# Four edits to a fused RWKV and two-layer MLP kernel: product order, place of the weight tests, form of mish, and the planner's distances

## The chip, the cores and the metric

The kernel runs on one core of a Trainium2 chip. The metric is device time of that core in microseconds (us): the median of three runs of the kernel before is 1250.47 us (1247.47 to 1251.25). Five engines work side by side, each with its own instruction stream in program order: PE (matrix products), DVE (vector), ACT (scalar functions), POOL and SP, which here issues all data movement. They meet through semaphores.

## The reference, cut to what matters

Three stages follow each other: a recurrence over 768 steps for 4 batches x 8 heads with a 40 x 40 state, a dense layer pair with mish, and a second pair with h - tanh(h). Weights come in float64.

```python
for t in range(S):                      # S = 768
    y[:, :, t] = einsum('bhd,bhde->bhe', rt, state)
    Sa = einsum('bhde,bhe->bhd', state, at)
    state_decay = state * wt[:, :, None, :] - einsum('bhd,bhe->bhde', Sa, bt)
    state = state_decay + einsum('bhd,bhe->bhde', vt, kt)
# tokens 3072, model width 320, hidden width 2048
h = x @ w_in;  x1 = (h * tanh(log1p(exp(h)))) @ w_out        # first layer
h = x1 @ w_in2; out = (h - tanh(h)) @ w_out2                 # second layer
```

## The kernel before

The work is in two phases. **Phase 1** takes the 768 steps as 12 chunks of 64. For each chunk and batch, `a0` and `a1` prepare scaled keys and a triangular matrix, `inv` inverts it, and `steps` makes the chunk's outputs and the new state with small matrix products: z, then the u products (`put` and `pu`, 16 of them for each chunk and batch, 768 in all, each of 64 rows of the array), then the state update. The 256 tokens of a finished chunk go through `moe1`, the first layer: 16 hidden blocks ("units"), in groups of four. `unit_in` makes h of a unit in PSUM (8 products), ACT takes a sigmoid of it into `th`, DVE multiplies h by it into `u`; `act` then runs an arctangent and a sine over the four units' `th`, and `unit_out` forms the activation, splits it in a high and a low part (`gh`, `gl`) and makes 6 products into y. There are 192 units. Arctangent and sine lie in different function tables, so each of the 48 groups brings table loads on ACT. Only two PSUM buffers hold h.

Beside this, phase 1 converts the float64 weights of the second layer in 88 pieces of 128 x 128 (`second_pieces`, `convert`, tile `raw`) and writes them to DRAM. With each piece `small` runs a test whether a value lies outside the range that the conversion can treat: an absolute value, a Relu with a sum into a column of `bad`, and the read of the accumulator, all on ACT, on the same buffer that DVE goes on to use.

**Phase 2** is the second layer: 6 blocks of 512 tokens, 16 units each, 20 products a unit (8 into h, 12 from its activation). In its first two blocks it also reads the decay `w` (8 loads) and the first layer's weights (20 loads of 512 KB into two buffers `wax`) and tests them on ACT. If any test hits, a general version runs at the end; otherwise it is skipped.

The order on every engine is set by a planner (`Plan`), which records all operations and runs a list scheduling with estimated costs (`cost`), a delay from the end of an operation to its dependents on another engine (`lat`, 150 or 200 ns), and a time for a load to land (`LAND`, 850 ns, more for some). An operation recorded with `nc.copy` may stand on ACT or on DVE, as the planner finds. The planner also keeps a running sum of PE's columns and puts in idle products (`warm`) in the first two chunks. Its numbers are its own estimates, and no time here is taken from them.

In the profile all instructions have one line (L277), that of the planner's call; they are told apart by the names of tiles.

Of the kernel before, what the change touches and what calls it, by code (L numbers as in the profile page):

```python
# [9 lines left out]
F32 = mybir.dt.float32  # L10
F32R = mybir.dt.float32r
U32 = mybir.dt.uint32
AF = mybir.ActivationFunctionType
# [12 lines left out]
NF = DFF // 128  # L26
TB = B * C
SETS = 2 * B
NBAD = 117
SW = 1.0  # L30
PEN2 = 0
CUT = 16
# [50 lines left out]
class Plan:  # L83
# [11 lines left out]
    DUTY0 = 4500  # L95
    DRAIN = 95
    NEAR = 600
    LAND = 850

    def __init__(self, nc):  # L100
        self.nc, self.tasks, self.acc, self.open, self.fused, self.weight = nc, [], {}, None, False, 1.0
# [40 lines left out]
    @staticmethod  # L142
    def cost(engine, method, out, ins, kw):
        n = math.prod(out.shape[1:])
        if engine == "tensor":
            m = math.prod(ins[0].shape[1:])
            k = ins[0].shape[0]
            if method == "transpose":
                return max(0.43 * n + 10, 0.83 * m + 4) if k > 64 else max(0.43 * n + 6, 0.42 * m + 8)
            if ins[1].dtype == F32R:  # L150
                return max(0.43 * n + 10, 0.83 * m + 4)
            if max(k, m) > 64 and m > 64:
                return 2 * max(0.83 * n + 5, 0.83 * m + 5)
            if k <= 32:
                return 22 if m <= 16 or n <= 16 else 45
            return max(0.83 * n + 6, 0.83 * m + 5)
        if engine == "vector":
            if method == "reciprocal":
                return 69 + 6 * n
            if method == "tensor_tensor_scan" or method == "transpose" and len(out.shape) > 3:  # L160
                return 69 + n / 0.48
            fast = method in ("tensor_scalar", "tensor_copy") and all(a.space != PSUM for a in ins)
            return 69 + n / (1.92 if fast else 0.96)
        if engine == "scalar":
            more = sum(isinstance(kw.get(x), bass.AP) for x in ("bias", "scale", "accum_out"))
            return (51 if kw["in_"].space == PSUM else 93) + 93 * more + n / 1.2
        if engine == "gpsimd":
            return 149 + 2.1 * n if method == "tensor_tensor" else 70 + 0.8 * n
        return 600

    def add(self, engine, method, args, kw, *more):
# [33 lines left out]
        if engine == "sync":  # L205
            run = min(16384, 4 * min(self.contiguous(out), *(self.contiguous(a) for a in ins)))
            packets = math.prod(out.shape) * 4 / run
            t["size"] = packets * max(10, 5 + 0.05 * run) / 16
            far = ins[0].space == DRAM and (run >= 4096 or run <= 256 and packets > 1000)
            t["fixed"] = self.LAND + 1000 * far  # L210
            t["late"] = 700 + t["fixed"] + t["size"]
            rows, local = out.shape[0], out.space != DRAM and ins[0].space != DRAM
            issue = {128: 400, 64: 640, 40: 330 if packets <= 80 else 814, 32: 632 if local else 449, 24: 822}.get(rows, 633)
            t["alts"][engine] = issue + 30, t["alts"][engine][1]
        for ap, write in [(a, a.space == PSUM) for a in ins] + [(o, True) for o in outs]:
            name, p0, p1, lo, hi = self.region(ap)
            ws, rs = self.acc.setdefault(name, ([], []))
            for old, raw in ((ws, True), (rs, False)) if write else ((ws, True),):
                for q0, q1, l, h, o in old:
                    if q0 < p1 and p0 < q1 and l < hi and lo < h and o is not t:  # L220
                        if o["alts"].keys() == t["alts"].keys() and len(t["alts"]) == 1:
                            lat = 60 if raw and engine == "vector" else 0
                        else:
                            lat = 200 if "tensor" in o["alts"] else 150
                        t["preds"][o["id"]] = max(t["preds"].get(o["id"], 0), lat)
            if write:
                for old in (ws, rs):
                    old[:] = [x for x in old if not (p0 <= x[0] and x[1] <= p1 and lo <= x[2] and x[3] <= hi)]
                ws.append((p0, p1, lo, hi, t))
            else:  # L230
                rs.append((p0, p1, lo, hi, t))
# [380 lines left out]
def fused(ctx, tc, cs, odd, wax0, rv0, wax, rv, vn, cst, w, win1, wout1, win2, wout2, out):  # L612
# [45 lines left out]
        nc.scalar.activation(out=mk, in_=mk, func=AF.Abs)  # L658
        count(mk, mk, amin, -1.0)

    def convert(dst, raw, fh, check):

        lo, hi = raw[..., 0], raw[..., 1]
        nc.vector.tensor_scalar(
            out=fh, in0=hi, scalar1=0x07FFFFFF, scalar2=3, op0=ALU.bitwise_and, op1=ALU.logical_shift_left)
        nc.vector.scalar_tensor_tensor(
            out=fh, in0=hi, scalar=0xC0000000, in1=fh, op0=ALU.bitwise_and, op1=ALU.bitwise_or)
        lf, mk = lo.bitcast(F32), hi.bitcast(F32)
        nc.scalar.activation(out=lf, in_=lo, func=AF.Copy, scale=2.0 ** -52)
        if check:  # L670
            small(mk)
        p2 = hi
        nc.vector.tensor_scalar(out=p2, in0=fh, scalar1=0xFF800000, scalar2=None, op0=ALU.bitwise_and)
        if dst.dtype == F32R:
            nc.tt(dst, p2.bitcast(F32), lf, ALU.mult)
            return
        nc.tt(p2.bitcast(F32), p2.bitcast(F32), lf, ALU.mult)
        nc.tt(dst, fh.bitcast(F32), p2.bitcast(F32), ALU.add)
# [22 lines left out]
    def load_first(win, wout, big, small, low, accs, eyes):  # L701
# [5 lines left out]
        def piece(q, raw, parts):  # L707


            n = raw.shape[1]  # L710
            fh = small()[:, 0:n]
            s = fh.bitcast(F32)
            m = low()[:, 0:n]
            convert(m if q < QPE else s, raw, fh, False)

            def like(t, hi):
                return t.rearrange("p (z n) -> p z n", z=hi.shape[1]) if len(hi.shape) == 3 else t

            for hi, lo, r, c in parts:
                x = like(s[:, c], hi)  # L720
                nc.copy(hi, x)
                if q >= QPE:
                    nc.tt(lo, x[r], hi[r].bitcast(F32), ALU.subtract)
            if q < QPE:
                acc = accs[next(count) % NACC][:, 0:n]
                nc.cut()
                nc.tensor.matmul(acc, ident, s, start=True, stop=False)
                nc.tensor.matmul(acc, eyes[0], m, start=False, stop=False)
                for hi, lo, r, c in parts:
                    nc.tensor.matmul(acc[:, c], eyes[1], hi, start=False, stop=c.stop == n)  # L730
                for hi, lo, r, c in parts:
                    nc.copy(lo, like(acc[:, c], hi)[r])
# [36 lines left out]
    def second_pieces(win, wout):  # L769
        def piece(load, store, dup):  # L770
# [1 line left out]
            load(raw)  # L772
            fh = st.tile([128, 128], U32, tag="fh", name="fh", bufs=1)
            s = fh.bitcast(F32)
            convert(s, raw, fh, True)
            r = raw.rearrange("p n k -> p (n k)").bitcast(F32).rearrange("p (k n) -> p k n", k=2)
            hi, lo = r[:, 0], r[:, 1]
            nc.copy(hi.bitcast(F32R), s)
# [46 lines left out]
    with ExitStack() as p1:  # L825
# [277 lines left out]
        def steps(c, bs, xt, vuc):  # L1103
# [45 lines left out]
            for i in turn:  # L1149
                pg = psB(ns[i])  # L1150
                pus[i, 0] = pg[64:128, 0:NP * D], slice(64, 128)
                puts[i, 0] = pg[:, 256:256 + 2 * C]

                r = slice(64 * i, 64 * i + 64)
                pus[i, 1] = b3[r, 0:NP * D], r
                puts[i, 1] = b3[:, 160 + 2 * C * i:160 + 2 * C * i + 2 * C]
            nc.cut()
            for g in range(2):
                q = slice(64 - 64 * g, 128 - 64 * g)
                for i in turn:  # L1160
                    pu = pus[i, g][0].rearrange("p (h d) -> p h d", d=D)
                    put = puts[i, g].rearrange("p (k t) -> p k t", t=C)
                    for h in range(NP):
                        z0 = 64 * (h % 2)
                        nc.tensor.matmul(put[z0:z0 + D, h // 2, :], zs[i][q, h, :], Xs[i][q, h, :], start=True, stop=True)
                        nc.tensor.matmul(pu[:, h, :], Xs[i][q, h, :], zs[i][q, h, :], start=True, stop=True)
            for g in range(2):
                q = slice(64 - 64 * g, 128 - 64 * g)
# [103 lines left out]
        def moe1(c, x, wts):  # L1272
# [15 lines left out]
            def unit_in(f, th, u):  # L1288
# [13 lines left out]
                nc.tensor.matmul(h, w2[:, fc], t2[:, 0], start=False, stop=False)  # L1302
                nc.tensor.matmul(h, w2[:, fc], t2[:, 1], start=False, stop=True)
                nc.scalar.activation(out=th, in_=h, func=AF.Sigmoid, bias=bln2)
                nc.vector.tensor_tensor(out=u, in0=h, in1=th, op=ALU.mult)

            def act(ths):

                with nc.fuse():
                    for th in ths:  # L1310
                        nc.scalar.activation(out=th, in_=th, func=AF.Arctan)
                    for th in ths:
                        nc.scalar.activation(out=th, in_=th, func=AF.Sin, bias=bpi2, scale=-2.0)

            def unit_out(f, th, u):
                nc.vector.scalar_tensor_tensor(out=u, in0=th, scalar=1.0, in1=u, op0=ALU.add, op1=ALU.mult)
                gh = ap.tile([128, TB], F32R, tag="gh", name="gh", bufs=2)
                nc.copy(gh, u)
                gl = ap.tile([128, TB], F32R, tag="gl", name="gl", bufs=2)
# [159 lines left out]
        for i in range(8):  # L1479
# [1 line left out]
            nc.sync.dma_start(out=t, in_=w[:, i])  # L1481
            nc.scalar.activation(out=t, in_=t, func=AF.Abs, bias=mid)
            count(t, t, edge, 1.0)
        for win in (win1, wout1):
            flat = win.bitcast(U32).rearrange("r c -> (r c)").rearrange("(p n k) -> p n k", p=128, k=2)
            for i in range(10):
                t = t_wax[i % 2][:, 0:1024].bitcast(U32).rearrange("p (n k) -> p n k", k=2)
# [187 lines left out]
```

## Time and profile before

| | us |
|---|---|
| median of three runs | 1250.47 |
| the profiled execution | 1259.04 |
| its span, first to last instruction | 1257.1 |
| PE busy | 1182.5 (94%) |
| DVE busy | 948.1 (75%) |
| ACT busy | 814.6 (65%) |
| granted TensorE clock, mean share of full | 0.970 |

Phase 1 lasts from the start to 892 us, when the first product of phase 2 starts; the first layer's units run from about 128 us on. PE's busy time is that of pipelined products whose ends are modelled, so a high share does not say that PE is full: products of 0.31 us duration often start 0.15 us apart.

### The profile page before, as it was taken

What the parts mean: (1) busy time and instruction counts of PE and PEld (TensorE: products, weight loads), DVE (VectorE), ACT (ScalarE), POOL (GpSimd) and SP (SyncE); (2) the same over time, 40 slices, a digit from 0 to 9 for tenths busy, and PEclk for the clock granted to TensorE, in tenths of its full rate; (3) what the DMA queues carried; (4) which work ended last, traced back from release to release, by engine and by line L of the source; (5) the groups of instructions that cost most, each with busy time, mean ns of one, the idle gap of its engine ahead of it and who ended that gap; (6) DMA issues with size and microseconds to landing.
All of it is one profiled execution on the core that took longest, in us unless ns stands there. A gap on an engine that the chain in (4) does not pass through costs nothing. (4 is left out here: it accounts for less than half of the span.)

```text
span 1257.1 us, 38131 instructions
## 1 busy us (share of the span) xinstructions
PE 1182.5 (94%) x15289; PEld 1082.5 (86%) x15289; DVE 948.1 (75%) x2904; ACT 814.6 (65%) x1855; POOL 21.5 (2%) x78
## 2 busy tenths in 40 slices
PE   8899898999999989899899999999999999999996
PEld 7789797889898989888788898889988999999996
DVE  8889897879989888888798997878755454544542
ACT  3564866777878786867678787889785653333332
POOL 1000000000000000000000000000000000000000
PEclk9999998999999989998999988999999999999999
DMA  9457243344343434253443534335865550200001
GB/s 267 131 157 157 63 95 84 99 94 107 77 114 82 115 68 101 64 124 69 96 109 92 128 87 95 74 81 122 279 212 139 171 127 1 47 1 22 5 17 24
DMA packets 253041, 125.61 MB, mean 100 GB/s; under 512 B 190520, under 2 KB 238136, under 8 KB 252856
## 3 DMA queue, kind: packets, MB, share of 16 engines
q1 hardware_dynamic: 252856, 123.09, 39.1%
q8 instruction: 122, 2.00, 0.7%
q14 instruction: 63, 0.52, 0.1%
HBM read 91.58 MB, written 26.61 MB: 94 GB/s over the span
## 5 line engine op out<-in xcount | busy, mean ns | idle before, releaser
L277 PE MATMUL y<-wo,gh 128*128 128x320 f32 (+1 forms) x902 | 214.2, 323 | 3.6 <-DVE gh L277 2.6
L277 PE MATMUL h<-xt,wih 128*128 128x256 f32 (+1 forms) x800 | 181.9, 319 | 7.3 <-DVE u L277 5.9
L277 PEld LDWEIGHTS y<-wo,gh 128*128 128x128 f32 x902 | 151.3, 193 | 12.0 <-DVE gh L277 4.6
L277 PEld LDWEIGHTS h<-xt,wih 128*128 128x128 f32 x800 | 132.0, 200 | 13.8 <-DVE u L277 7.7
L277 PE MATMUL y<-wo,gl 128*128 128x320 f32 x448 | 141.4, 316 | 2.6 <-DVE fh L277 1.3
L277 ACT ACT_TABLE_LOAD x98 | 125.7, 1283 | 4.9 <-DVE u L277 2.4
L277 PE MATMUL h<-xt,wil 128*128 128x256 f32 (+1 forms) x400 | 122.6, 306 | 0.7 <-issue 0.7
L277 PE MATMUL h<-t,wi 128*128 128x256 f32 (+1 forms) x448 | 103.8, 314 | 2.8 <-DMA t<-xs 2.8
L277 ACT ACTIVATE th<-h,cs 128x256 f32<-128x256 f32 x168 | 76.7, 470 | 35.5 <-PE h L277 34.1
L277 PEld LDWEIGHTS y<-wo,gl 128*128 128x128 f32 x448 | 86.1, 192 | 6.8 <-DVE gl L277 5.0
L277 DVE SCALAR_TENSOR_TENSOR u<-th,u 128x256 f32<-128x256 f32 (+2 forms) x187 | 78.5, 441 | 7.3 <-ACT th L277 6.8
L277 PEld LDWEIGHTS h<-t,wi 128*128 128x128 f32 x448 | 76.2, 200 | 7.3 <-DMA t<-xs 2.5
L277 PEld LDWEIGHTS h<-xt,wil 128*128 128x128 f32 x400 | 80.3, 201 | 2.0
L277 ACT ACTIVATE rv<-ps 128x128 f32<-128x128 f32 (+1 forms) x132 | 49.3, 384 | 49.9 <-PE ps L277 48.0
L277 DVE TENSOR_TENSOR gl<-u,gh 128x256 fp32r<-128x256 f32 x176 | 73.1, 416 | 4.5 <-ACT gh L277 2.3
L277 DVE TENSOR_TENSOR u<-h,th 128x256 f32<-128x256 f32 x164 | 66.7, 415 | 10.6 <-ACT th L277 10.0
L277 DVE TENSOR_TENSOR x<-h,rv 128x512 f32<-128x512 f32 x48 | 33.1, 690 | 52.2 <-ACT rv L277 51.8
L277 DVE TENSOR_TENSOR x<-ps,rv 128x512 f32<-128x512 f32 x48 | 33.1, 690 | 52.0 <-ACT rv L277 52.0
L277 DVE TENSOR_TENSOR t<-t 128x15 f32<-128x15 f32 (+4 forms) x360 | 70.9, 197 | 1.5
L277 DVE TENSOR_TENSOR lt<-ps,cs 128x512 f32<-128x512 f32 x96 | 65.3, 683 | 6.2 <-PE ps L277 5.8
L277 ACT ACTIVATE th<-th 128x1024 f32<-128x1024 f32 (+2 forms) x63 | 58.7, 933 | 8.7 <-DVE u L277 7.3
L277 PE MATMUL ps<-z,x 64*64 64x40 f32 x768 | 63.1, 220 | 0.0
(224 smaller groups left out, 2928.2 us busy)
## 6 DMA issues: line engine op xcount, KB each, us to landing
wax<-in_wax_dram SPq DMA_DIRECT2D x88, 160.8 KB
rv<-in_rv_dram SPq DMA_DIRECT2D x92, 64.0 KB
dm<-lt SPq DMA_DIRECT2D x22, 256.0 KB
x<-dx SPq DMA_DIRECT2D x22, 256.0 KB
wo<-w2o SPq DMA_DIRECT2D x8, 640.0 KB
wax<-in_win_dram SPq DMA_DIRECT2D x10, 512.0 KB
wax<-in_wout_dram SPq DMA_DIRECT2D x10, 512.0 KB
lt<-x1d SPq DMA_DIRECT2D x144, 32.0 KB
```

Source lines behind the costliest of these rows:

```text
L277: getattr(getattr(self.nc, engine), method)(*args, **kw)
```

## The change

Four edits:

1. The u products of a chunk and batch were recorded first for the one half of the array's rows and then for the other; now the halves take turns, product by product. The two halves write different PSUM banks, as before.
2. The test of the second layer's weights leaves `convert`; phase 2 reads the two float64 matrices again, with 20 more loads of 512 KB and their tests, as it does for the first layer's. `bad` has 56 columns for 117.
3. mish: with s the sigmoid of h - ln 2, the factor was 1 + sin(pi/2 - 2 arctan s), multiplied with h s; now it is sin(2 arctan s), multiplied with h. So DVE's product of h and the sigmoid becomes a copy of h out of PSUM, which may stand on either engine; the sine loses its bias operand; and a three-operand DVE instruction becomes a two-operand one.
4. The planner's numbers: `LAND` 850 to 1500, 3000 more for loads into `raw`, 300 for 150 from another engine to PE, and 110 more for ACT and DVE operations with fewer than 128 output rows.

```diff
-    LAND = 850
+    LAND = 1500
+    TOPE = 300
+    SECOND = 3000
+        part = 110 if out.shape[0] < 128 and method != "transpose" else 0
-            return 69 + n / (1.92 if fast else 0.96)
+            return 69 + part + n / (1.92 if fast else 0.96)
...
-                            lat = 200 if "tensor" in o["alts"] else 150
+                            lat = 200 if "tensor" in o["alts"] else self.TOPE if engine == "tensor" else 150
...
-        if check:
-            small(mk)
...
-            for g in range(2):
-                q = slice(64 - 64 * g, 128 - 64 * g)
-                for i in turn:
-                    for h in range(NP):
-                        nc.tensor.matmul(put[z0:z0 + D, h // 2, :], zs[i][q, h, :], Xs[i][q, h, :], start=True, stop=True)
-                        nc.tensor.matmul(pu[:, h, :], Xs[i][q, h, :], zs[i][q, h, :], start=True, stop=True)
+            for i in turn:
+                for h in range(NP):
+                    for g in range(2):
+                        nc.tensor.matmul(put[z0:z0 + D, h // 2, :], zs[i][q, h, :], Xs[i][q, h, :], start=True, stop=True)
+                    for g in range(2):
+                        nc.tensor.matmul(pu[:, h, :], Xs[i][q, h, :], zs[i][q, h, :], start=True, stop=True)
...
-                nc.vector.tensor_tensor(out=u, in0=h, in1=th, op=ALU.mult)
+                nc.copy(u, h)
-                        nc.scalar.activation(out=th, in_=th, func=AF.Sin, bias=bpi2, scale=-2.0)
+                        nc.scalar.activation(out=th, in_=th, func=AF.Sin, scale=2.0)
-                nc.vector.scalar_tensor_tensor(out=u, in0=th, scalar=1.0, in1=u, op0=ALU.add, op1=ALU.mult)
+                nc.tt(u, th, u, ALU.mult)
...
-        for win in (win1, wout1):
+        for win in (win1, wout1, win2, wout2):
```

The order of the built program shows what the planner made of it. First PE, the u products of chunk 1 (`x` and `z` are the operands; `ps_141` takes the results of one half of the rows, `ps_144` those of the other). Before:

```order
L277 MATMUL ps_141<-x_134,z_125 40x64
L277 MATMUL ps_141<-z_125,x_134 64x40
L277 MATMUL ps_141<-x_134,z_125 40x64
L277 MATMUL ps_141<-z_125,x_134 64x40
L277 MATMUL ps_141<-x_134,z_125 40x64
L277 MATMUL ps_141<-z_125,x_134 64x40
L277 MATMUL ps_141<-x_134,z_125 40x64
L277 MATMUL ps_141<-z_125,x_134 64x40
L277 MATMUL ps_144<-x_134,z_125 40x64
L277 MATMUL ps_144<-z_125,x_134 64x40
```

The same place on PE in the changed program:

```order
L282 MATMUL ps_141<-x_134,z_125 40x64
L282 MATMUL ps_144<-x_134,z_125 40x64
L282 MATMUL ps_141<-z_125,x_134 64x40
L282 MATMUL ps_144<-z_125,x_134 64x40
L282 MATMUL ps_141<-x_134,z_125 40x64
L282 MATMUL ps_144<-x_134,z_125 40x64
L282 MATMUL ps_141<-z_125,x_134 64x40
L282 MATMUL ps_144<-z_125,x_134 64x40
```

Each product of one half is now followed by its twin of the other half; the 16 products still stand in one piece.

Second ACT, the hundredth unit or so of the first layer (`th` sigmoid, arctangent, sine; `h` the unit's result in PSUM; `raw` a weight piece). Before:

```order
L277 ACTIVATE th_166<-h_147,cs 128x256
L277 ACTIVATE th_166<-h_148,cs 128x256
L277 ACTIVATE vu_120<-ps_144 64x160
L277 ACTIVATE gh_169<-u_149 128x256
L277 ACTIVATE raw_206<-raw_206 128x128 x2
L277 ACTIVATE raw_206,bad<-raw_206,cs 128x128
L277 ACTIVATE th_166<-h_147,cs 128x256
L277 ACTIVATE rv_122<-ps_142 128x2x64
```

The hundredth unit on ACT in the changed program:

```order
L282 ACTIVATE th_166<-h_147,cs 128x256
L282 ACTIVATE xt_168<-ah_195 128x2x64
L282 ACTIVATE u_149<-h_147 128x256
L282 ACTIVATE th_166<-h_148,cs 128x256
L282 ACTIVATE z_126<-ps_142 128x160
L282 ACTIVATE u_149<-h_148 128x256
L282 ACTIVATE z_125<-ps_141 128x160
L282 ACTIVATE raw_204<-raw_204 128x128
```

Of a piece's four ACT rows the scaling stays and the two rows of the test (with the read of its sum) are gone; the copy of h stands on ACT one or two rows behind the sigmoid of the same h. Over the whole program 135 of the 192 copies stand on ACT and 57 on DVE; of the 135, 51 stand directly behind their sigmoid, 69 with one row between them and 15 further back. Table loads are as many as before.

Third ACT in the third block of phase 2 (`rv` is the tanh of a unit, `wax` the buffer of a test). Before, there is no test left there:

```order
L277 ACTIVATE rv_122<-ps_143 128x512
L277 ACTIVATE gh_170<-x_135 128x256
L277 ACTIVATE rv_122<-ps_144 128x512
L277 ACTIVATE xt_168<-x_135 128x512
L277 ACTIVATE rv_121<-h_147 128x512
```

The third block on ACT in the changed program:

```order
L282 ACTIVATE rv_122<-ps_143 128x512
L282 ACTIVATE wax_117<-wax_117 128x512
L282 ACTIVATE wax_117,bad<-wax_117,cs 128x512
L282 ACTIVATE gh_170<-x_135 128x256
L282 ACTIVATE rv_122<-ps_144 128x512
L282 ACTIVATE xt_168<-x_135 128x512
L282 ACTIVATE wax_116<-wax_116 128x512
L282 ACTIVATE wax_116,bad<-wax_116,cs 128x512
L282 ACTIVATE rv_121<-h_147 128x512
```

About one test stands between two tanh there. The tests, 13, 14 and 1 of them in the first three blocks before, now stand 12 each in the first four.

## Rows read from the trace of the kernel before

**Rows 1.** Stretches: length, busy PE, PEld, DVE, ACT, POOL, clock, DMA share, GB/s.

```profile
128.00:892.00 764.00, 713.28 (x11870) 661.59 (x11858) 652.99 (x2223) 583.30 (x1363) 15.66 (x58) 0.96 0.41 97
...
957.00:1015.00 58.00, 57.59 (x320) 52.20 (x321) 30.17 (x60) 36.01 (x76) 0.00 (x0) 1.00 0.55 152
1015.00:1072.50 57.50, 57.50 (x322) 52.08 (x320) 28.53 (x56) 23.40 (x46) 0.00 (x0) 1.00 0.18 37
```

**Rows 2.** The chain that ended last: start, length, engine and tile, products.

```profile
802.09 2.11 PE h L277 x16
...
809.54 1.74 PE y L277 x12
...
957.41 3.70 PE h L277 x15
...
1014.94 3.66 PE h L277 x16
...
1072.43 3.66 PE h L277 x16
```

**Rows 3.** Waits of DVE, 128 to 892 us: us in total, times, longest.

```profile
DVE u L277 <- ACT th L277: 16.9, 25, 2.2
DVE fh L277 <- DMA raw<-in_wout_dram: 15.8, 9, 5.2
DVE raw L277 <- ACT raw L277: 15.6, 32, 1.0
```

**Rows 4.** Waits of PE, the same stretch.

```profile
PE h L277 <- DVE u L277: 5.9, 7, 1.6
```

**Rows 5.** Groups of one shape: busy us, mean ns, idle before and its releasers.

```profile
L277 DVE TENSOR_TENSOR u<-h,th 128x256 f32<-128x256 f32 x164 | 66.7, 415 | 10.6 <-ACT th L277 10.0
L277 DVE SCALAR_TENSOR_TENSOR u<-th,u 128x256 f32<-128x256 f32 x168 | 66.0, 417 | 7.3 <-ACT th L277 6.8
...
L277 ACT ACTIVATE th<-th,cs 128x1024 f32<-128x1024 f32 x44 | 50.6, 1151 | 0.5
...
L277 ACT ACTIVATE th<-th 128x1024 f32<-128x1024 f32 x44 | 46.3, 1053 | 7.9 <-DVE u L277 7.3 <-DVE wax L277 0.3
...
L277 ACT ACTIVATE gh<-u 128x256 fp32r<-128x256 f32 x106 | 43.0, 410 | 14.3 <-PE y L277 10.7 <-DVE u L277 1.8 <-DVE gl L277 0.5
...
L277 ACT ACTIVATE kn<-ps 128x320 f32<-128x320 f32 x49 | 21.1, 431 | 9.2 <-PE ps L277 9.0
...
L277 DVE COPY kn<-ps 128x320 f32<-128x320 f32 x11 | 5.3, 481 | 0.4 <-PE ps L277 0.4
```

**Rows 6.** DVE in order of time: two of the products in turn.

```profile
437.75 0.74 DVE L277 TENSOR_TENSOR u<-h,th 128x256 f32<-128x256 f32 x2
```

**Rows 7.** ACT in order of time: a weight piece's test, and what follows it.

```profile
897.86 0.31 ACT L277 ACTIVATE raw<-raw 128x128 f32<-128x128 f32 x1
898.21 0.41 ACT L277 ACTIVATE raw<-raw,cs 128x128 f32<-128x128 f32 x1
...
898.61 0.58 ACT L277 ACTIVATE rv<-h 128x512 f32<-128x512 f32 x1
```

**Rows 8.** PE in order of time: one set of u products, first, last, next.

```profile
410.53 0.25 PE L277 MATMUL ps<-x,z 64*40 64x64 f32 x1
...
411.48 0.37 PE L277 MATMUL ps<-z,x 64*64 64x40 f32 x4
411.78 0.56 PE L277 MATMUL y<-wo,gh 128*128 128x320 f32 x2
```

**Rows 9.** PE in order of time: chunk 0's z products, in which the halves take turns.

```profile
71.50 0.66 PE L277 MATMUL ps<-vu,lt 64*64 64x40 f32 x16 [0.35 <-ACT x L277]
72.09 1.12 PE L277 MATMUL h<-u,cs 128*128 128x512 f32 x2
```

**Rows 10.** ACT in order of time: a test in phase 2, and what follows it.

```profile
985.18 0.68 ACT L277 ACTIVATE wax<-wax 128x512 f32<-128x512 f32 x1 [0.44 <-DMA wax<-in_win_dram]
...
986.64 0.58 ACT L277 ACTIVATE rv<-h 128x512 f32<-128x512 f32 x1
```

More of the change, by code (lines that the diff above doesn't have):

```diff
@@ L28 @@
 SETS = 2 * B
-NBAD = 117
+NBAD = 56
 SW = 1.0
@@ L162, in cost @@
             fast = method in ("tensor_scalar", "tensor_copy") and all(a.space != PSUM for a in ins)
-            return 69 + n / (1.92 if fast else 0.96)
+            return 69 + part + n / (1.92 if fast else 0.96)
         if engine == "scalar":
             more = sum(isinstance(kw.get(x), bass.AP) for x in ("bias", "scale", "accum_out"))
-            return (51 if kw["in_"].space == PSUM else 93) + 93 * more + n / 1.2
+            return (51 if kw["in_"].space == PSUM else 93) + part + 93 * more + n / 1.2
         if engine == "gpsimd":
@@ L210, in add @@
             t["fixed"] = self.LAND + 1000 * far
+            if ins[0].space == DRAM and out.name.startswith("raw"):
+                t["fixed"] += self.SECOND
             t["late"] = 700 + t["fixed"] + t["size"]
@@ L659, in small, with convert @@
         count(mk, mk, amin, -1.0)
-    def convert(dst, raw, fh, check):
+    def convert(dst, raw, fh):
         lo, hi = raw[..., 0], raw[..., 1]
@@ L667, in convert @@
             out=fh, in0=hi, scalar=0xC0000000, in1=fh, op0=ALU.bitwise_and, op1=ALU.bitwise_or)
-        lf, mk = lo.bitcast(F32), hi.bitcast(F32)
+        lf = lo.bitcast(F32)
         nc.scalar.activation(out=lf, in_=lo, func=AF.Copy, scale=2.0 ** -52)
-        if check:
-            small(mk)
         p2 = hi
@@ L713, in piece @@
             m = low()[:, 0:n]
-            convert(m if q < QPE else s, raw, fh, False)
+            convert(m if q < QPE else s, raw, fh)
             def like(t, hi):
@@ L774, in piece @@
             s = fh.bitcast(F32)
-            convert(s, raw, fh, True)
+            convert(s, raw, fh)
             r = raw.rearrange("p n k -> p (n k)").bitcast(F32).rearrange("p (k n) -> p k n", k=2)
@@ L1157, in steps @@
             nc.cut()
-            for g in range(2):
-                q = slice(64 - 64 * g, 128 - 64 * g)
-                for i in turn:
-                    pu = pus[i, g][0].rearrange("p (h d) -> p h d", d=D)
-                    put = puts[i, g].rearrange("p (k t) -> p k t", t=C)
-                    for h in range(NP):
-                        z0 = 64 * (h % 2)
+            for i in turn:
+                for h in range(NP):
+                    z0 = 64 * (h % 2)
+                    for g in range(2):
+                        q = slice(64 - 64 * g, 128 - 64 * g)
+                        put = puts[i, g].rearrange("p (k t) -> p k t", t=C)
                         nc.tensor.matmul(put[z0:z0 + D, h // 2, :], zs[i][q, h, :], Xs[i][q, h, :], start=True, stop=True)
+                    for g in range(2):
+                        q = slice(64 - 64 * g, 128 - 64 * g)
+                        pu = pus[i, g][0].rearrange("p (h d) -> p h d", d=D)
                         nc.tensor.matmul(pu[:, h, :], Xs[i][q, h, :], zs[i][q, h, :], start=True, stop=True)
```

## The prediction

> **What bounds the kernel now.** I read the stretches first, then the waits and the single groups, and the chain last. From 957 us on the kernel is bound by PE: it is busy 57.5 of 57.5 us while DVE has 28.5 and ACT 23.4 [rows 1], and the chain is nothing but products, a block every 57.5 us [rows 2]. Phase 1 is another matter. From 128 to 892 us PE is busy 713 of 764 us, DVE 653, ACT 583 [rows 1], and PE's figure is the one to distrust: it is made of products that overlap. By start-to-start times 16 products into h take 2.11 us and 12 into y 1.74 us [rows 2], so a unit of the first layer (8 and 6) costs 1.06 + 0.87 = 1.93 us and all 192 cost 370 us; the scan's small products fill part of the rest, at about 1.25 us for a set of u products [rows 8]. DVE's 653 us (85%) are instructions in strict order, and its largest waits are for ACT and for loads [rows 3], short ones. ACT's 583 us (76%) come second. So I take phase 1 as held by DVE, with ACT close behind. There is no chain to prove it: the one shown reaches back only over the last part of phase 1. That is the main uncertainty here.
>
> **Mish.** DVE loses 192 products of h and sigmoid. One lasts 0.415 us [rows 5], but two in turn take 0.74 us, so the second starts 0.74 - 0.415 = 0.33 us after the first [rows 6]: 192 x 0.33 = 63 us of DVE's issue time. The order gives 57 copies back to DVE. The trace has no copy of this shape from PSUM; the 128x320 one takes 0.481 us [rows 5], the removed product of 256 columns 0.415, so I take the same 0.33: +19. The three-operand instruction at 0.417 becomes a two-operand one, of which the trace shows 0.415 [rows 5]: nothing. DVE: -63 + 19 = -44 us. ACT gains 135 copies. The nearest row is the `gh` copy of the same shape, 0.41 us alone [rows 5]; less the 0.08 us by which neighbours overlap, as on DVE, 0.33: +45 us (with 0.41, +55). The sine without its bias goes from 1.15 to the 1.05 us of the arctangent [rows 5]: 48 x 0.10 = -5 us.
>
> The Trainium skill speaks against this move ("ScalarE: Activation LUTs", section on rules for kernel authors: plain multiplications and additions belong on VectorE, which is quicker per element). For a source in PSUM the trace does not agree: 128x320 takes 0.431 us on ACT and 0.481 on DVE [rows 5]. By the page all 192 copies would sit on DVE, its 44 us would be no gain, and about 16 us would be left of the whole sum below.
>
> **The weight tests.** A test on ACT starts with its absolute value at 897.86 and the next instruction starts at 898.61: 0.75 us [rows 7]. 88 of them are -66 us on ACT, nearly all in phase 1. So ACT as a whole has -66 + 45 - 5 = -26 us in phase 1. DVE gains by this too: it goes on with the same buffer only after the test, which is its 15.6 us of waiting for `raw` [rows 3]. A later copy no longer waits for the sigmoid either; of the 16.9 us behind `th`, 10.0 belong to that product [rows 3, 5]. Both may vanish (-25.6) or be replaced by the next wait in line (0); I take half, -13.
>
> Phase 2 gets 20 more tests and 10 MB of loads. One takes 986.64 - 985.18 = 1.46 us of ACT [rows 10], 29 us in all. The cover is PE's products: ACT is busy 36 of 58 us in the block with tests and 23.4 of 57.5 in the one without [rows 1], and the block with tests took 1014.94 - 957.41 = 57.53 us against 57.49 without [rows 2]. Behind a test that waits for its load stand a tanh and the split of g, and PE waits for these; the row shows such a wait of 0.44 us [rows 10], and the block lost 0.04. Were the cover gone, 20 x (1.46 + 0.44) = 38 us. I take +1.
>
> **The u products.** A set takes 411.78 - 410.53 = 1.25 us to the next product. Its 32 passes (two for each product) last about 0.23 us each, so the last of them starts at 411.48 + 0.37 - 0.23 = 411.62, and they start 1.09 / 31 = 35 ns apart [rows 8]. In chunk 0's z products, also of 64 rows and 40 columns, the halves already take turns: 16 passes within 0.66 us, (0.66 - 0.23) / 15 = 29 ns apart [rows 9]. At that pace a set saves 31 x 6 ns = 0.2 us, 48 sets 9 us of PE. Ends: 0, if nothing changes, and 48 x 0.55 = 26 us if two halves run wholly beside each other. I take the row, and of its 9 us only 4 on the path, since PE does not hold phase 1.
>
> The Trainium skill ("TensorE: Matmul & The Clock Gate", part on packing small matmuls, section on the mechanism) has a weight load overlap a running product only when their row groups differ, and tiles starting about 4 ns apart. That would put this order at the 26 us end. The chunk 0 rows show 29 ns a pass on average, so the page's pace is not reached there.
>
> **The planner's distances.** They add no instruction. They should shorten waits for loads, of which the 15.8 us for second-layer pieces is the largest [rows 3], and may as well let an engine idle that has something ready. From -16 to +16; I take -5. SP's queue holds loads and stores in one order, so a piece that comes later also stores later, but 88 pieces in 890 us leave it room.
>
> **The sum.** DVE is relieved of 44 + 13 = 57 us of 653. If that became time one for one, ACT, with 557 us left, would soon stand beside DVE's 596, and two engines that feed each other are not both kept at 85%. I count 0.65 of it: -37. With u products -4, distances -5, tests +1: -45 us. The profiled execution took 1259.04 us (span 1257.1, 1.9 us around it), so it would take 1214; the median of the runs lies 8.6 us lower, at 1250.5, so I forecast 1205.
>
> **Rivals.**
> - *All of it counts.* DVE keeps its 85% share: 44 / 0.85 = 52, both waits gone 26, u products 9, less 10 for what overlaps: about -77, 1174. For it: PE has slack by start-to-start times. Against: ACT is close. 0.15.
> - *The scan's own chain sets the pace,* not DVE: each chunk waits for the state of the one before, through z, u products, two copies and the update, and what DVE saves turns into idle time. Then only u products (9) and some waits (3) count: 1238. For it: DVE already idles 111 of 764 us. Against: none of its waits is large [rows 3]. 0.17.
> - *The copy holds up the h buffers (slower).* There are two PSUM buffers for h. Before, DVE freed one, and PE waited 5.9 us in all for that [rows 4]. Now 69 of the 135 ACT copies stand behind an instruction of another chain (a copy of `ah` or z) that may wait itself; ACT's waits for PE and DVE in the groups shown are near 0.1 to 0.2 us on average [rows 5]. PE then waits for the bank, and late products make later sigmoids late. The price decides at 45 / 69 = 0.65 us for each such copy; at 0.9 us it costs 62 us, and the kernel comes out at 1205 + 62 = 1267. Against: so long an average is several times what the rows show. 0.06.
> - *The turns do nothing:* if row halves do not overlap, the time is 1209, inside the forecast's range.
>
> **How the numbers follow.** The forecast, 1190 to 1225, gets 0.57; the rivals 0.15, 0.17 and 0.06; no change to within 0.3% (3.8 us, about what a measurement here can tell) 0.05. Faster: 0.57 + 0.15 + 0.16 = 0.88, since a little of the chain case ends at no change; same 0.06, slower 0.06. The range 1174 to 1240 holds the forecast, most of the chain case and half of the full one.
>
> **What would show it.** The start of phase 2 moves from 892 to about 850 us and its blocks still take 57.5 us; DVE's busy time falls by about 60 to 70 us while its share of phase 1 falls little; its waits for `raw` and `th` shrink; u products start 29 ns apart. I am wrong if phase 1 keeps its length with DVE idle more (the chain), if PE's waits for `u` grow to tens of us (the buffers), or if blocks with tests take over 59 us.

## The result, and the profile after

The changed kernel takes 1209.0 us (median of four runs, 1205.3 to 1215.5) against 1250.9 for the kernel before: a ratio of 0.9653, interval 0.9619 to 0.9688, so 42 us less. The profiled execution took 1215.45 us.

The stretches come first, as in [rows 1] (length, then busy time of PE, PEld, DVE, ACT and POOL, granted clock as a share of the full 2.4 GHz, DMA share, GB/s). The first row is phase 1 from 128 us to the first product of phase 2, the others are blocks of phase 2.

```profile
128.00:852.41 724.41, 681.84 (x11838) 636.17 (x11821) 609.67 (x2086) 563.93 (x1256) 13.17 (x58) 0.96 0.43 103
913.00:971.00 58.00, 58.00 (x326) 52.58 (x325) 28.09 (x55) 35.85 (x75) 0.00 (x0) 1.00 0.49 135
971.00:1028.50 57.50, 57.50 (x322) 52.08 (x322) 27.91 (x54) 35.56 (x73) 0.00 (x0) 1.00 0.49 136
1086.00:1143.50 57.50, 57.50 (x322) 52.08 (x321) 27.88 (x54) 21.36 (x42) 0.00 (x0) 1.00 0.05 13
```

Phase 1 is 39.6 us shorter (764.0 before). DVE's busy time fell by 43.3 us, ACT's by 19.4. DVE's idle time, which is the length less the busy time, hardly moved: 111.0 before, 724.41 - 609.67 = 114.7 now. The blocks with tests have 14 us more on ACT than the one without and the same length. The chain of waits shows that too (start, length, engine and tile, products; compare [rows 2]):

```profile
913.95 3.66 PE h L282 x16
971.44 3.65 PE h L282 x16
1028.92 3.66 PE h L282 x16
1086.41 3.66 PE h L282 x16
1143.89 3.66 PE h L282 x16
```

Every step is 57.5 us, with tests or without. The first block, in which phase 1 runs out, became 2.8 us shorter: by the first products of the blocks it lasted from 891.77 to 956.00 us before, and now from 852.41 to 913.79. So 42.2 us of the span's gain of 43.4 were made by the end of that block. The rest is a wait at the start of the second block, which is gone now. Before, its first two products stood like this (start, length, in brackets the idle time before and who ended it):

```profile
956.00 0.49 PE L277 MATMUL h<-xt,wih 128*128 128x512 f32 x1 [0.51 <-ACT xt L277]
957.41 0.50 PE L277 MATMUL h<-xt,wih 128*128 128x512 f32 x1 [0.91 <-DVE xt L277]
```

DVE's waits in phase 1 (us in total, times, longest), against [rows 3]:

```profile
DVE x L282 <- ACT x L282: 13.8, 18, 2.3
DVE isc L282 <- DMA x1d<-isc: 12.9, 8, 6.1
DVE u L282 <- ACT th L282: 11.4, 20, 1.0
DVE lt L282 <- PE ps L282: 8.1, 13, 1.2
DVE isc L282 <- PE y L282: 7.7, 6, 2.4
DVE gl L282 <- ACT gh L282: 5.3, 13, 0.8
DVE raw L282 <- ACT raw L282: 5.2, 13, 1.0
...
DVE fh L282 <- DMA raw<-in_wout_dram: 0.3, 1, 0.3
```

The three waits of [rows 3] went from 48.3 to 16.9 us in all (`th` 11.4, the load 0.3, `raw` 5.2). What came in their place is spread over five other rows of the list, `x`, the two `isc`, `lt` and `gl`: 23.1 us before, 47.8 now.

PE waited for the copies of h on ACT, which answers to [rows 4]:

```profile
PE h L282 <- ACT u L282: 2.7, 4, 1.4
```

And the groups of one shape (busy us, mean ns of one, idle before), beside [rows 5]:

```profile
L282 ACT ACTIVATE th<-th 128x1024 f32<-128x1024 f32 x88 | 93.3, 1060 | 1.8
...
L282 DVE TENSOR_TENSOR u<-th,u 128x256 f32<-128x256 f32 x168 | 66.8, 414 | 5.8 <-ACT th L282 5.6
...
L282 ACT ACTIVATE u<-h 128x256 f32<-128x256 f32 x122 | 44.8, 379 | 0.1
...
L282 DVE COPY u<-h 128x256 f32<-128x256 f32 x46 | 19.0, 416 | 5.8 <-ACT th L282 5.7
```

ACT copies h in 379 ns where DVE takes 416, with 0.1 us of idle time ahead of all its copies together. DVE's copies still wait 5.7 us for the sigmoid: in the planner's code a read of PSUM counts as a write, so that the copy is put behind the sigmoid of the same h, though it uses none of its values. Arctangent and sine now form one group with one price, 1060 ns.

Last a set of u products (first, last, next), against [rows 8]:

```profile
402.42 0.25 PE L282 MATMUL ps<-x,z 64*40 64x64 f32 x2
...
402.99 0.29 PE L282 MATMUL ps<-z,x 64*64 64x40 f32 x4
403.21 1.16 PE L282 MATMUL ps<-az,wax 128*128 128x128 f32 x8
```

From the set's start to the next product it is 403.21 - 402.42 = 0.79 us, 1.25 before. By the working of the prediction the last pass starts at 402.99 + 0.29 - 0.23 = 403.05, so the 32 passes start 0.63 / 31 = 20 ns apart, not 35. The set is a typical one: the median from the start of a set to the next product is 1.25 us before and 0.79 now.

### The profile page after: what moved, and what is told of

Same layout as the page of the kernel before. It is cut to its first block, busy times and chain, and to the rows that moved or that the text cites. A ratio compares the mean times of both kernels' runs of the same rounds, so it can differ in the third digit from the quotient of the medians.

```text
span 1213.7 us, 38107 instructions
## 1 busy us (share of the span) xinstructions
PE 1150.1 (95%) x15321; PEld 1057.2 (87%) x15321; DVE 900.7 (74%) x2769; ACT 817.1 (67%) x1785; POOL 18.2 (1%) x79
## 3 DMA queue, kind: packets, MB, share of 16 engines
q1 hardware_dynamic: 255736, 133.58, 43.3%
## 4 chain that ended last, share of the span: by engine, by line
PE 49%; DVE 7%; ACT 3%; issue 2%; DMA 1%; SPq 1%; DVEq 0%; ACTq 0%
PE ps L282 25%; PE y L282 12%; PE h L282 12%; DVE t L282 2%; ACT th L282 1%; DVE u L282 1%; DMA x1d<-isc 1%; DMA t<-dm 1%; SPq L282 1%; DVE lt L282 1%; ACT L282 1%; DVE isc L282 1%; DVE gl L282 1%; DVE raw L282 0%; DVE fh L282 0%
## 5 line engine op out<-in xcount | busy, mean ns | idle before, releaser
L282 ACT ACTIVATE th<-th 128x1024 f32<-128x1024 f32 (+2 forms) x107 | 105.7, 988 | 4.2 <-DMA th<-in_wout_dram 2.3
L282 ACT ACTIVATE th<-h,cs 128x256 f32<-128x256 f32 x168 | 77.4, 471 | 33.9 <-PE h L282 32.8
L282 DVE TENSOR_TENSOR u<-th,u 128x256 f32<-128x256 f32 x168 | 66.8, 414 | 5.8 <-ACT th L282 5.6
L282 PE MATMUL h<-zr 128*128 128x256 f32 x496 | 68.7, 293 | 0.0
L282 PEld LDWEIGHTS h<-zr 128*128 128x128 f32 x496 | 63.8, 197 | 1.4
```

Source lines behind the costliest of these rows:

```text
L282: getattr(getattr(self.nc, engine), method)(*args, **kw)
```

## The experiments

The kernels of each group were timed on one chip together with the kernel before; ratios are to that (medians of it 1254.8 for the edits alone, 1255.9 for the edits undone, 1258.0 for the distances; the first row of the table is from the comparison above). Times in us; "idle" is the stretch from 128 us to the first product of phase 2 less DVE's busy time in it; the last column adds up what DVE and ACT waited there for loads of second-layer pieces (`raw`). Stretch, busy, idle and waits come from one profiled execution each, which lies up to 9 us from its kernel's median, so that differences of a few us in these columns say little.

| kernel | ratio and interval | median | stretch | DVE busy | idle | waits for `raw` loads |
|---|---|---|---|---|---|---|
| before | 1 | 1250.9 | 764.0 | 653.0 | 111.0 | 27.0 |
| mish alone | 0.9926 (0.9888-0.9965) | 1243.9 | 748.5 | 614.5 | 133.9 | 16.3 |
| tests alone | 0.9956 (0.9927-0.9985) | 1249.8 | 753.9 | 648.7 | 105.2 | 43.3 |
| u products alone | 0.9975 (0.9942-1.0009) | 1250.2 | 761.5 | 652.3 | 109.2 | 31.2 |
| distances alone | 0.9915 (0.9886-0.9945) | 1244.4 | 750.1 | 641.7 | 108.4 | 0.5 |
| changed | 0.9653 (0.9619-0.9688) | 1209.0 | 724.4 | 609.7 | 114.7 | 0.3 |
| without mish | 0.9744 (0.9710-0.9779) | 1224.5 | 734.4 | 641.0 | 93.4 | 0 |
| without tests' move | 0.9654 (0.9611-0.9696) | 1210.2 | 715.7 | 612.6 | 103.1 | 0 |
| without u products | 0.9719 (0.9680-0.9759) | 1222.5 | 734.1 | 612.1 | 122.0 | 0.7 |
| without distances | 0.9910 (0.9877-0.9943) | 1245.3 | 756.2 | 608.7 | 147.5 | 23.6 |
| old load distances | 0.9843 (0.9777-0.9909) | 1238.4 | 750.3 | 620.6 | 129.7 | 43.0 |
| old distance to PE | 0.9661 (0.9593-0.9728) | 1211.3 | 721.5 | 609.4 | 112.1 | 1.3 |
| no 110 for few rows | 0.9726 (0.9676-0.9775) | 1221.9 | 732.0 | 605.9 | 126.1 | 0 |
| all distances longer | 0.9644 (0.9590-0.9698) | 1212.4 | 725.9 | 607.9 | 118.0 | 3.6 |

The granted clock differs from run to run, and small effects cannot be told from it. Of the 21 runs of the kernel before beside the first four edits, the two at a mean clock of 0.984 took 1242.3 and 1245.9 us, the three at 0.964 and 0.967 between 1255.5 and 1258.9. Their median is 0.973; the runs with the tests' move alone have 0.979 and those with the distances alone 0.982. So part of these two gains of 5 and 11 us may go with the clock.

**One edit alone, on the kernel before.** First mish:

```diff
-                nc.vector.tensor_tensor(out=u, in0=h, in1=th, op=ALU.mult)
+                nc.copy(u, h)
...
-                        nc.scalar.activation(out=th, in_=th, func=AF.Sin, bias=bpi2, scale=-2.0)
+                        nc.scalar.activation(out=th, in_=th, func=AF.Sin, scale=2.0)
...
-                nc.vector.scalar_tensor_tensor(out=u, in0=th, scalar=1.0, in1=u, op0=ALU.add, op1=ALU.mult)
+                nc.tt(u, th, u, ALU.mult)
```

> The kernel before with the new mish alone. Theory 1 (DVE holds phase 1): DVE loses some 45 us of issue time and its waits for the sigmoid, ACT gains the copies but keeps the tests, so less moves to ACT: 25 to 35 us faster, near 1220. Theory 2 (PE's products hold phase 1): under 10 us, near 1243. Theory 3 (ACT's tests hold it): ACT only gets more work here, no gain, 1245 to 1260.

It brought 0.74%, 9 us. The stretch shows DVE relieved by 38.5 us, and ACT, which still has the tests, at 613.6 us, as busy as DVE:

```profile
128.00:876.45 748.45, 701.44 (x11693) 650.75 (x11693) 614.51 (x2111) 613.62 (x1481) 16.34 (x58) 0.97 0.42 100
```

and DVE's wait for the tests on ACT rose from 15.6 us [rows 3]:

```profile
DVE raw L277 <- ACT raw L277: 26.3, 43, 2.3
```

Less work on DVE alone turned mostly into idle time (133.9 us for 111.0). Theory 1 missed by 16 us or more. The gain has the size that theory 2 gave, that PE's products hold phase 1; the u products below speak against that theory.

Next the tests:

```diff
-        if check:
-            small(mk)
...
-        for win in (win1, wout1):
+        for win in (win1, wout1, win2, wout2):
```

> The kernel before with the second layer's tests in phase 2 alone. Theory 1: ACT is relieved of 66 us in phase 1 and DVE of up to 15.6 us of waiting for the piece's buffer, but DVE's work stays: 5 to 10 us faster, near 1243. Theory 2: nothing, 1251. Theory 3: most of the gain, 20 us or more, near 1228. Phase 2 costs at most 1 us in each theory.

It brought 0.44%, 5.5 us. This is the size of theory 1, less what goes with the clock. Here the waits of DVE show one wait partly in the place of another: the wait for the test went from 15.6 to 3.0 us, and those for the loads of the same pieces from 21.4 to 28.1, with a longest one of 7.1.

```profile
DVE fh L277 <- DMA raw<-in_win_dram: 15.0, 7, 7.1
DVE fh L277 <- DMA raw<-in_wout_dram: 13.1, 8, 4.2
...
DVE raw L277 <- ACT raw L277: 3.0, 8, 0.6
```

Then the u products:

```diff
+            for i in turn:
+                for h in range(NP):
...
+                    for g in range(2):
...
+                        nc.tensor.matmul(put[z0:z0 + D, h // 2, :], zs[i][q, h, :], Xs[i][q, h, :], start=True, stop=True)
```

> The kernel before with the u products by turns alone. In the changed kernel a set of 32 passes takes 0.79 us to the next product instead of 1.25, so 48 x 0.46 = 22 us of PE. Theory 1 (PE has slack in phase 1): 3 to 8 us faster, near 1246. Theory 2: nearly all 22 us, near 1230. Theory 3: under 8 us.

Alone they are not told apart from nothing (interval up to 1.0009): some 3 us of time for 22 us of PE's, where theory 2 wanted nearly all 22. The sets take 0.79 us here too, so that the order of the products alone makes their pace.

And the planner's numbers:

```diff
-    LAND = 850
+    LAND = 1500
+    TOPE = 300
+    SECOND = 3000
...
+        part = 110 if out.shape[0] < 128 and method != "transpose" else 0
```

> The kernel before with the planner's new distances alone; no instruction is added or removed. Theory 1: 0 to 8 us faster, near 1246, with shorter waits of DVE for pieces (15.8 and 5.6 us before). A theory 4, that order and not work was what changed: 15 us or more.

They brought 0.85%, 10.7 us, as much as mish and between theories 1 and 4. The waits for `raw` loads fell from 27.0 to 0.5 us, yet DVE's idle time only from 111.0 to 108.4; what fell is its busy time, by 11.3 us, since the planner placed other instructions on ACT:

```profile
128.00:878.14 750.14, 706.91 (x11879) 655.69 (x11879) 641.74 (x2188) 585.26 (x1350) 14.24 (x58) 0.97 0.41 99
```

Added up by who ended them, DVE's waits for transfers went from 29.1 to 7.4 us, and those for PE from 14.6 to 32.5. Here too another wait came in the place of the one that was removed. The four alone multiply to 0.977, 28 us; together they are worth 42.

**One edit undone in the changed kernel.** Each diff is one of those above turned round.

```diff
-                nc.copy(u, h)
+                nc.vector.tensor_tensor(out=u, in0=h, in1=th, op=ALU.mult)
```

> The changed kernel with the old mish. The four edits alone gave 9, 5, 3 and 11 us, 28 of about 44 together, so some help each other. Theory A (DVE and ACT hold phase 1 together: the copies pay only where ACT has been relieved of the tests): the new mish is worth 20 us or more here, ratio to before 0.980 to 0.985. Theory B (the edits add up, and the rest is the luck of one schedule): 9 us, ratio 0.972 to 0.975.

Mish as the last edit is worth 0.9744 - 0.9653 = 0.9%, 11 us (5 to 18, both intervals taken in quadrature, as in what follows). That is theory B's size, not the 20 us of theory A. DVE's busy time rose by 31.3 us and the stretch by 10 only; ACT fell to 532.6:

```profile
128.00:862.37 734.37, 687.65 (x11736) 636.31 (x11734) 640.95 (x2192) 532.60 (x1129) 14.05 (x58) 0.97 0.42 100
```

With the loads on time DVE can stand at 641 of 734 us, with an idle time of 93.4 that no other kernel here reached.

```diff
+        if check:
+            small(mk)
...
-        for win in (win1, wout1, win2, wout2):
+        for win in (win1, wout1):
```

> The changed kernel with the second layer's tests back in phase 1. Theory A: the tests' 66 us on ACT meet the copies there, so taking them out is worth 15 to 20 us with the new mish, against 5 alone: ratio to before 0.977 to 0.982, and ACT's share of phase 1 rises to about 82%, as in the run with mish alone. Theory B: 5 us, ratio 0.968 to 0.971.

No difference (within 7 us either way), less than either theory gave. ACT has 34 us more in phase 1, and PE a higher granted clock there than in the changed kernel (0.99 for 0.96):

```profile
128.00:843.65 715.65, 679.50 (x11789) 629.50 (x11789) 612.57 (x2099) 598.26 (x1445) 15.14 (x58) 0.99 0.44 105
```

The clock was higher in all four of its runs (0.979 to 0.990 over the whole, for 0.974 to 0.979), so a cost of the tests of a few us may be hidden in that; this stays open.

```diff
-            for i in turn:
-                for h in range(NP):
...
+            for g in range(2):
+                q = slice(64 - 64 * g, 128 - 64 * g)
+                for i in turn:
...
```

> The changed kernel with the u products half by half as before. Theory A: PE has slack in phase 1, 3 to 6 us, ratio to before 0.968 to 0.971, with sets of 1.25 us to the next product again. Against it: with DVE and ACT relieved, PE's 22 us begin to count, 10 us or more, ratio over 0.973.

The turns as the last edit are worth 0.66%, 8 us (2 to 15), between the two forecasts; the sets take 1.25 us again, and DVE has the same work to within 3 us and 7 us more idle time.

```diff
-    LAND = 1500
-    TOPE = 300
-    SECOND = 3000
+    LAND = 850
...
-        part = 110 if out.shape[0] < 128 and method != "transpose" else 0
```

> The changed kernel with the planner's old distances. Theory A and B: about what they gave alone, 8 to 12 us, ratio to before 0.972 to 0.976. Against it: the gain alone was one lucky order, and here it is under 4 us, ratio under 0.969.

This is the run that decides, and no theory had its size. All three edits of the work are there, and only 0.9% is left of 3.5%; the distances as the last edit are worth 32 us (26 to 38). Stretch and DVE's waits:

```profile
128.00:884.16 756.16, 689.56 (x11692) 638.33 (x11693) 608.68 (x2080) 567.28 (x1272) 19.31 (x58) 0.95 0.42 99
```

```profile
DVE fh L277 <- DMA raw<-in_wout_dram: 14.8, 7, 4.0
DVE lt L277 <- PE ps L277: 14.6, 14, 3.0
...
DVE gl L277 <- ACT gh L277: 12.4, 18, 2.3
```

DVE's and ACT's busy times are those of the changed kernel to within 4 us, and phase 1 is 31.8 us longer: all of it is idle time of DVE, 147.5 for 114.7. The loads of pieces hold 20.8 us of this; `lt` and `gl`, which wait for engines that themselves came late, hold 14 more than in the changed kernel. Added up by who ended them, DVE's waits for transfers are 38.0 us here and 23.3 in the changed kernel, those for ACT 50.1 and 44.7, those for PE 38.2 and 29.6: with the three other edits in place all three sums are smaller with the distances, where alone one fell and another rose.

**The distances one by one, in the changed kernel.** First those of the loads:

```diff
-    LAND = 1500
+    LAND = 850
...
-    SECOND = 3000
+    SECOND = 0
```

> The changed kernel with the old landing time for loads (LAND 850, nothing more for second-layer pieces), the other distances new. All distances old cost 32 us (ratio 0.991 against 0.965), and with them DVE waits 21 us for pieces in phase 1, against 0.3. Theory C (each distance removes the waits that it names): 15 to 22 us lost, ratio 0.977 to 0.984, and the waits for pieces are back at about 20 us. Theory D (any other order of the planner moves the time by about 10 us either way, and the tried numbers are a lucky draw): ratio 0.967 to 0.980 with no link to those waits.

They are worth 1.9%, 24 us (14 to 33): the upper end of theory C, and by the value, though not by the whole interval, above the range of theory D. The waits for pieces are twice what C gave, 25.3 us on DVE and 17.7 on ACT. Of the 25.9 us by which the stretch is longer, though, only 15.0 are idle time of DVE; 10.9 are work, which the planner placed on it instead of on ACT:

```profile
128.00:878.34 750.34, 692.31 (x11981) 639.71 (x11980) 620.63 (x2101) 559.85 (x1256) 15.91 (x59) 0.96 0.42 100
```

DVE's waits for loads, and ACT's:

```profile
DVE fh L282 <- DMA raw<-in_win_dram: 13.3, 7, 5.8
...
DVE fh L282 <- DMA raw<-in_wout_dram: 12.0, 10, 2.5
```

```profile
ACT raw L282 <- DMA raw<-in_win_dram: 8.9, 4, 3.2
ACT raw L282 <- DMA raw<-in_wout_dram: 8.8, 4, 3.7
```

The longest of them, in order of time: the issue on SP, and what both engines do (start, length, instruction, in brackets the idle time before it and who ended it).

```profile
477.85 0.36 SPq L282 DMA_DIRECT2D raw<-in_win_dram  x1
...
481.82 0.32 ACT L282 ACTIVATE raw<-raw 128x128 f32<-128x128 uint32 x1 [2.33 <-DMA raw<-in_win_dram]
481.83 0.23 DVE L282 TENSOR_SCALAR fh<-raw 128x128 uint32<-128x128 uint32 x1 [5.84 <-DMA raw<-in_win_dram]
```

SP issued the load 4.0 us before the piece was used, and DVE, which has its order fixed, stood with the piece as its next work for 5.84 us, while ACT stood for 2.33. By its code the planner counts 700 ns, `LAND` and about 450 for the size, which with 850 is 2.0 us, half of that. This load is among the slow ones: nearly all those that an engine waited for in this run took 2.2 to 4.9 us from issue to use. And 1.9 of the 5.84 us passed before the load was issued, since SP itself waited 2.1 us for the store of an earlier piece (`w2i<-raw`, issued at 473.80). `LAND` stands for stores too. What `LAND` and what the 3000 for pieces is worth by itself was not tried.

Then the delay to PE:

```diff
-    TOPE = 300
+    TOPE = 150
```

> The changed kernel with 150 again from another engine to PE. Theory C: PE's and its weight loads' waits in phase 1 go back towards 67 and 101 us from 41 and 70, 8 to 15 us lost, ratio 0.972 to 0.978, waits for pieces stay near zero. Theory D: as for any other order, within 10 us either way.

Worth nothing (1 us, within 9 either way). Theory C failed here: the waits that this distance names did not come back, 35.8 us on PE and 63.0 on its weight loads, less than the 41 and 70 of the changed kernel.

```diff
-        part = 110 if out.shape[0] < 128 and method != "transpose" else 0
+        part = 0 if out.shape[0] < 128 and method != "transpose" else 0
```

> The changed kernel without the 110 more for operations with fewer than 128 rows. Theory C: the estimate is nearer to the trace with it, but no wait is named by it: 0 to 6 us lost, ratio 0.965 to 0.970. Theory D: within 10 us either way.

Worth 0.7%, 9 us (2 to 17): there is no wait for pieces, but DVE idles 11 us more. Theory C gave at most 6 us, and 9 is what theory D allows. The trace shows no price of few rows that the 110 would stand for; copies of 160 columns out of PSUM in the changed kernel, with 64 and with 128 rows:

```profile
L282 ACT ACTIVATE vu<-ps 64x160 f32<-64x160 f32 x71 | 21.1, 297 | 14.5 <-PE ps L282 13.5
L282 ACT ACTIVATE sn<-ps 128x160 f32<-128x160 f32 x30 | 8.5, 296 | 2.4 <-PE ps L282 2.3
L282 DVE COPY vu<-ps 64x160 f32<-64x160 f32 x25 | 8.0, 321 | 1.7 <-PE ps L282 1.1
L282 DVE COPY sn<-ps 128x160 f32<-128x160 f32 x14 | 4.3, 313 | 2.1 <-PE ps L282 2.1
```

They take nearly the same time, 297 and 296 ns on ACT, 321 and 313 on DVE. By its code the planner counts 184 and 236 ns for both; the 110 brings it near the trace for 64 rows and leaves it as far off for 128. So it makes good a shortfall of small copies for some of them, and is no price of few rows.

```diff
-    LAND = 1500
-    TOPE = 300
-    SECOND = 3000
+    LAND = 1700
+    TOPE = 340
+    SECOND = 3400
```

> The changed kernel with its three distances 13% longer (1700, 3400, 340). Theory C: the waits are already gone, so the time stays within 4 us of the changed kernel, ratio 0.962 to 0.969. Theory D: a new draw, up to 10 us slower, ratio up to 0.973, or quicker.

The same time as the changed kernel (within 8 us either way), as theory C gave. Three new orders were tried in which no or hardly any wait for pieces came back: two moved the time by 1 us, within 8 and 9, and one by 9. So the theory that any new order moves it by up to ten us is not excluded, but the 32 us of all distances and the 24 (14 to 33) of the loads' are beyond ten. No version tried was clearly quicker than the changed kernel.

## Why the prediction came out

The forecast of 1205 us was right in its number, and in the place of the gain: phase 1 shortened, and phase 2 held its pace. The start of phase 2 came at 852 us (about 850 forecast). But the way to the number was wrong in its main terms, and that they made up for each other was luck. By the sum the three edits of the work bring 40 us (37, 4, less 1) and the distances 5; without the distances the three bring 11 us, and the distances add 32.

- *What bounds phase 1.* DVE's work is the larger part of it but does not set its length alone. Mish by itself took 38.5 us of work from DVE and 15.5 off the stretch, and in the changed kernel 31.3 for 10. In these runs DVE, relieved, waited more as long as what it waited for came no earlier. That PE's products alone hold it is out by the 3 to 8 us that 22 us of them brought.
- *Mish, -44 us on DVE.* Phase 1 shows -43.3 for all four edits, -38.5 for this one alone and -31.3 for it as the last. With each kernel the planner also places other copies anew, and these runs do not part that from the edit: the distances alone took 11.3 us off DVE, as the last edit they put 1.0 on it. The price of a copy on ACT was put at 0.33 us of issue; a single one takes 379 ns, 0.30 less the same 0.08. The step that copies go to ACT is borne out. The rule of the Trainium skill that was weighed against it is stated there for bf16 ("ScalarE: Activation LUTs", rules for kernel authors). For this f32 shape out of PSUM the trace shows the reverse: 379 ns on ACT, 416 on DVE. A copy was also to wait no longer for the sigmoid; those on DVE still wait 5.7 us for it.
- *The weight tests, half of 25.6 us of waits.* This step failed. The named waits did shrink, from 32.5 to 16.6 us, yet DVE's idle time did not (111.0 and 114.7). Alone, the edit took 12.6 us off the wait for tests, put 6.7 on the waits for loads and gained 5 us of time at a higher clock; undone in the changed kernel it cost nothing. That phase 2 takes the 20 tests at no cost was right. The 57.53 us read for the block with tests run from its second product, however; from the first, at 956.00, to that of the next block it was 58.8, so the reading did not show a cover as complete as it seemed. The rows after, 57.5 us with 12 tests in a block, do.
- *The u products, 29 ns a pass.* Mis-sized: 20 ns, so 48 x 0.46 = 22 us of PE and not 9. The chunk 0 rows [rows 9] were a poor neighbour. The 22 us are near the 26 us end, which the rule of the Trainium skill ("TensorE: Matmul & The Clock Gate", packing, the mechanism) spoke for, though the pace that it gives is not reached. That only part of it lies on the path was right: 3 us alone, 8 as the last edit, 4 forecast.
- *The planner's distances, -5 us.* This is the term that was mis-sized most: -10.7 alone and -32 as the last edit, twice the bound of 16. The loads' part of the 32 is 24. The prediction priced the wait that the trace before showed (15.8 us on one row [rows 3]) and took a third of it. It did not ask whether another wait stands behind that one. On DVE the distances end about 21 us of waits for pieces either way (21.4 before, 20.8 without the distances); alone, 2.6 us of idle time go with them, and in the changed kernel 32.8. So the wait itself had not grown; what changed is whether ending it lets DVE go on.
- *The factor of 0.65.* It gave -37 us for DVE's relief of 57 from mish and the tests. As last edits these two are worth 11 us and 0, alone 9 and 5: 11 to 14 us where the factor gave 37. For phase 1 the whole sum was -46 us, and 39.6 were measured; the distances made up for most of what this term lacked.
- *The signs.* The blocks kept 57.5 us, DVE's share of phase 1 fell little (85 to 84%), and its waits for `raw` and `th` shrank, as forecast. DVE's busy time fell by 43.3 us where 60 to 70 were to show it; that figure did not follow from the sum either, which takes 44 us of work off DVE, the other 13 being waits.

Of the rivals, "all of it counts" (1174) and the slower one are out. The h buffers made no stall: 2.7 us of waiting where the price would have decided at 45. "The turns do nothing" is out by the 20 ns. "The scan's own chain sets the pace" (1238) is out for the changed kernel, yet its sign, idle time in place of work, is what the kernel without distances shows, at 1245 us. Late loads of pieces, which the rival did not name, are 20.8 us of DVE's waits there; whether the scan's chain holds part of the rest was not tried.

Open: why the edits together bring 42 us and one by one 28, for which the runs show only that DVE's waits are exchanged in the one case and fall in the other; why the tests' move brings nothing as the last edit though ACT is 34 us lighter by it; and by which chain of waits the 110 ns for few rows gain their 9 us.

## What to carry to other kernels

Where a planner fixes the order, work taken from the busiest engine becomes time only if what that engine waits for can come earlier too. Add up its waits by who ended them before and after an edit, to see whether a wait was ended or exchanged, and compare the landing time that the plan assumes with the one in the trace (here 2.0 us planned, 2.2 to 4.9 for the loads that were waited for). Price such an edit together with the others, not by the wait before alone, and test it both ways: alone it was worth 11 us, as the last one 32.

## What was not expected of the hardware

- Products of 64 rows whose row halves take turns started 20 ns apart, 35 where one half comes after the other and 29 in chunk 0's z products; the order alone makes the difference in the first two, alone and in the changed kernel (0.79 and 1.25 us a set).
- A copy of 128x256 out of PSUM is quicker on ACT than on DVE (379 and 416 ns).
- Copies of 160 columns out of PSUM take as long with 64 rows as with 128 (297 and 296 ns on ACT, 321 and 313 on DVE).
- The four runs of the changed kernel follow the granted clock over the whole: 1215.5, 1211.4, 1206.6 and 1205.3 us at 0.974, 0.975, 0.978 and 0.979. In the profiled one the blocks of phase 2 stand at 1.00 and phase 1 at 0.96. What makes it vary from run to run was not tried.
